# Agent attention with a gated expert layer: a shorter way to the list of failed tokens, and the last answer laid among the last products

## The chip, the cores and the metric

The kernel runs on one core of a Trainium2 chip. The metric is the time of one execution on the device in microseconds (us), as the median of several runs. One core has a matrix engine (TensorE, PE in the profile, with PEld for its weight loads), three element-wise engines (VectorE or DVE, ScalarE or ACT, GpSimd or POOL), a sequencer that mostly issues transfers (SyncE or SP), and DMA queues. Each engine takes its own instructions in the order in which they are written, and engines wait for one another through semaphores.

## What is computed

There are 4 batches of 11456 tokens, 128 channels and 49 agents. Each token's row is routed to one of 8 experts and goes through that expert's two layers (128 to 1024 to 128). The reference, cut to what matters:

```python
def _attn_ref(q, k, v, agents):
    a2k = sm(agents, k);  agent_v = a2k @ v          # sm: scaled softmax of a @ b.T
    return sm(q, agents) @ agent_v
def _moe_ref(x, expert_emb, tau, w1, w2):            # x: all 45824 rows
    ...
    expert_idx = np.argmax(logits, axis=1)
    gate_w = probs[np.arange(N), expert_idx]
    for e in range(E):
        mask = expert_idx == e
        h = np.maximum(x[mask] @ w1[e], 0.0)
        out[mask] = gate_w[mask, None] * (h @ w2[e])
```

## The kernel before

**Batches and units.** For each batch the kernel reads k and v and forms the agents' values. It then guesses one expert for the whole batch (`pick_expert`) and folds that expert's first layer into the space of the 49 agent scores: `gh` and `gl` are the folded weights that are kept, `lin` holds what could be taken as linear, `w2p` the second layer. GpSimd makes a factor `gts` of these (L946, L948), and TensorE multiplies it into `linp` (L952). Query tokens go by in units of up to 8 tiles of 128. A unit's scores become exponentials `e` and, transposed, `tt`. From there the batch's own layers run: a pair of products `hp` (L1338, L1339) for four tiles, ACT's `hh` (L1347) and DVE's `hh` (L1348), then for each tile the products `lin` (L1361) and twelve triples `yp` (L1373 to L1375), and for each group of tiles DVE's gated `ot` (L1389) and a store on ACT's queue (L1395).

**Failed tokens.** The folded form is only good for a token that is of the batch's guessed expert and for which the hidden units that were left out behave as assumed. `proved` tests the second: products `vp` (L1182, L1185), a sum on ACT (L1191), a minimum on DVE (L1188), collected in `vmin` and `vsum`. Once all tests of a batch are seen, `mark_strays(b)` runs. It finds each token's expert (`idx`), marks failed tokens (`odd`), and of the failed ones with the batch's own expert takes up to 5 of each partition with one sort of the largest 8 (`top`). A product with a triangular matrix (`had`, L1246) counts how many lie in the partitions before, so each picked token gets one of 128 places. Five comparisons make one-hot masks `mput` (L1272), and five products `mine` (L1281) move number and gate to those places. `fix(b)` turns the numbers to row indices `ix` (L1500), gathers the 128 q rows by an indirect transfer on POOL (`gather`, L1422) and calls `answer`.

**The answer.** `answer` computes 128 tokens in full: transpose `sqT` (L1431), scores `ssp` (L1437), softmax, transpose `seT` (L1449), attention rows `sx` (L1456), the expert's first layer `shp` (16 products at L1473, relu `sh` on ACT), second layer `syp` (16 products, L1479), the gate (`so`, L1484), and a scatter on POOL over the rows already stored (L1487). Every step but the first layers of batch 3 can stand among another batch's products; `w1s` and `w2s` are loaded anew. Tokens of another expert are counted by groups (`lga` L1308, `cnt_p` L1311, the transposes `mT` and `mB` at L222 and L228, `left`) and answered by `stray`, and those beyond that in a device loop at the end, which is entered only if some are left.

**What sets the order.** All these parts are Python generators. `spawn` enters one in a list that is advanced at each step of the loop over TensorE's products, `yield n` waits n steps, `urgent(g, k)` advances g k times a step at a high priority, and `in_place(y_last)` makes the scheduler place a product behind the last own product written so far. So a change in a count of steps, or in when a generator is spawned, moves instructions on every engine.

Of the kernel before, what the change touches and what calls it, by code (L numbers as in the profile page):

```python
# [29 lines left out]
def kernel(ctx: ExitStack, tc: tile.TileContext, q, k, v, agents, emb, tau, w1, w2, out):  # L30
# [18 lines left out]
    KEEP = 5  # L49
    LATE = 16  # L50
# [280 lines left out]
    def setup():  # L331
# [4 lines left out]
        with tc.issue_after(turned[0].ins):  # L336
            pool.iota(iotaf, pattern=[[1, FV]], base=0, channel_multiplier=0, allow_small_or_imprecise_dtypes=True)
            pool.iota(uid, pattern=[[P, NF]], base=0, channel_multiplier=1)
            pmem(half, 0.5)
            pool.iota(iota8m, pattern=[[1, E]], base=64, channel_multiplier=0, allow_small_or_imprecise_dtypes=True)  # L340
            pool.iota(iota8n, pattern=[[1, E]], base=-LO, channel_multiplier=0, allow_small_or_imprecise_dtypes=True)
            pool.iota(pidx, pattern=[[0, 1]], base=0, channel_multiplier=1, allow_small_or_imprecise_dtypes=True)
            dve.tensor_scalar(tri, iotaf[:, :P], pidx, None, ALU.is_gt)
            dve.tensor_tensor(out=fold, in0=ident[:, :A], in1=ident[:, LO : LO + A], op=ALU.add)
            dve.tensor_reduce(out=mrow[:, :1], in_=fold, axis=AX.X, op=ALU.add)
            dve.tensor_scalar(mrow[:, 1:], mrow[:, :1], -1.0, 1.0, ALU.mult, ALU.add)
            pmem(iotah, -1.0)
            pool.tensor_copy(iotah[:, :P], iotaf[:, :P])
            pool.tensor_copy(iotah[:, P + XA :], iotaf[:, P:FN])
            pool.iota(tok[:, :, :J], pattern=[[N, B], [1, J]], base=0, channel_multiplier=J,  # L350
                      allow_small_or_imprecise_dtypes=True)
        yield 1
        with tc.issue_after(turned[0].ins):
            pool.iota(tok[:, :, J:], pattern=[[N, B], [1, REM_J]], base=P * J, channel_multiplier=REM_J,
                      allow_small_or_imprecise_dtypes=True)
        pmem(gid, -1.0)
# [378 lines left out]
    def pick_expert(b, g):  # L735
# [23 lines left out]
        dve.tensor_copy(bt.e0, e0i)  # L759
# [337 lines left out]
    def route_group(b, gi, n):  # L1097

        bt = batches[b]
        if gi == 0:  # L1100
            bt.lg = wk.tile([P, NCOL, E], F32, name="lga", tag="lga", bufs=1)
            bt.es = es_all[:, b, :]
            bt.l = sm.tile([P, NCOL], F32, name="la", tag="la")
            bt.vmin = sm.tile([P, NCOL], F32, name="vmin", tag="vmin")
            bt.vsum = sm.tile([P, NCOL], F32, name="vsum", tag="vsum")
            bt.seen = 0
            pmem(bt.vmin, BIG)
            pmem(bt.vsum, 0.0)
# [34 lines left out]
        act.activation(ex, lg, AF.Exp)  # L1143
        yield 1
# [55 lines left out]

    def mark_strays(b):

        bt = batches[b]
        while bt.seen < sum(len(checks(b, u)) for u in range(NU)):
            yield 1
        yield 2
        dve.scalar_tensor_tensor(out=bt.lg, in0=bt.lg, scalar=0.0, in1=iota8n.unsqueeze(1).broadcast_to([P, NCOL, E]),
                                 op0=ALU.is_equal, op1=ALU.mult)
        yield 1
        idx = sm.tile([P, NCOL], F32, name="idx", tag="idx", bufs=1)  # L1210
        dve.tensor_reduce(out=idx, in_=bt.lg, axis=AX.X, op=ALU.min)
        yield 1
# [3 lines left out]
        ne = sm.tile([P, NCOL], F32, name="ne", tag="ne", bufs=1)  # L1216
        dve.tensor_tensor(out=ne, in0=bt.l, in1=bt.l, op=ALU.mult)
        yield 1
        dve.scalar_tensor_tensor(out=ne, in0=bt.qq[:, 1], scalar=bt.far, in1=ne, op0=ALU.mult, op1=ALU.is_ge)
        yield 1  # L1220
        dve.scalar_tensor_tensor(out=odd, in0=bt.vmin, scalar=0.0, in1=ne, op0=ALU.is_lt, op1=ALU.max)
# [5 lines left out]
        dve.tensor_scalar(ne, idx, float(LO), bt.e0, ALU.add, ALU.not_equal)  # L1227
        yield 1
        dve.tensor_tensor(out=odd, in0=ne, in1=odd, op=ALU.is_lt)
        pmem(odd[REM_P:, J:], 0.0)  # L1230
        yield 1
        cand = sm.tile([P, NCOL], F32, name="mine", tag="mine", bufs=1)
        top = sm.tile([P, 8], F32, name="top", tag="top", bufs=1)
        had = sm.tile([P, 8], F32, name="had", tag="had", bufs=1)
        cnt = sm.tile([P, 1], F32, name="had1", tag="had1", bufs=1)
        c16 = sm.tile([P, 1], F16, name="had16", tag="had16", bufs=1)
        dve.scalar_tensor_tensor(out=cand, in0=tok[:, b], scalar=1.0, in1=odd, op0=ALU.add, op1=ALU.mult)
# [3 lines left out]
        dve.tensor_scalar(had[:, :KEEP], top[:, :KEEP], 0.0, 0.0, ALU.is_gt, ALU.add, accum_out=cnt)  # L1241
        yield 1
# [5 lines left out]
        own = sm.tile([P, 1], F32, name="had3", tag="had3", bufs=1)  # L1248
        dve.tensor_tensor(out=own, in0=t_[:, :1], in1=cnt, op=ALU.add)
        dve.tensor_copy(cnt, t_[:, :1])  # L1250
        yield 1
        dve.tensor_scalar(had[:, :KEEP], iotaf[:, :KEEP], cnt, None, ALU.add)
# [5 lines left out]
        pick = sm.tile([P, KEEP, 2], F32, name="mpick", tag="mpick", bufs=1)  # L1258
        dve.tensor_copy(pick[:, :, 0], top[:, :KEEP])
        yield 1  # L1260
        mg = sm.tile([P, NCOL], F32, name="mgate", tag="mgate", bufs=1)
        mj = bt.vmin
        dve.tensor_tensor(out=mg, in0=bt.es, in1=odd, op=ALU.mult)
        yield 1
        for i in range(KEEP):
            dve.scalar_tensor_tensor(out=mj, in0=cand, scalar=top[:, i : i + 1], in1=mg, op0=ALU.is_equal, op1=ALU.mult,
                                     accum_out=pick[:, i, 1:])
            yield 1
        parts = sm.tile([P, KEEP, 3, 2], F16, name="mparts", tag="mparts", bufs=1)
        puts = sm.tile([P, B * NCOL], F32, name="mput", tag="eq", bufs=1).bitcast(F16)[:, : KEEP * P].rearrange("p (k f) -> p k f", f=P)  # L1270
        for i in range(KEEP):
            dve.tensor_scalar(puts[:, i], iotaf[:, :P], had[:, i : i + 1], None, ALU.is_equal)  # L1272
        for i in range(3):
            pool.tensor_copy(parts[:, :, i], pick)
            if i < 2:
                pool.tensor_tensor(out=pick, in0=pick, in1=parts[:, :, i], op=ALU.subtract)
        yield 3
        t_ = pss("mine")
        with in_place(y_last):
            for i in range(KEEP):  # L1280
                pe.matmul(out=t_[:, :6], lhsT=puts[:, i], rhs=parts[:, i].rearrange("p i w -> p (i w)"), start=(i == 0), stop=(i == KEEP - 1))  # L1281
# [10 lines left out]
        spawn(fix(b), 1, half=True)  # L1292
# [134 lines left out]
    def answer(xq, ix, gt, aT, avn, w1s, w2s, tiles=0):  # L1427
# [62 lines left out]
    def fix(b):  # L1490
# [5 lines left out]
        none = sm.tile([P, 1], F32, name="none", tag="none", bufs=1)  # L1496
        ix = sm.tile([P, 1], I32, name="ix", tag="ix")
        dve.tensor_scalar(none, bt.fix[:, :1], 0.5, 2 * BIG, ALU.is_lt, ALU.mult)
        yield 1
        dve.scalar_tensor_tensor(out=ix, in0=bt.fix[:, :1], scalar=-1.0, in1=none, op0=ALU.add, op1=ALU.add)  # L1500
# [4 lines left out]
        yield from answer(xq, ix, bt.fix[:, 1:], aT_all[:, b], av_all[:, b], w1s, w2s, (b + 1) * NT)  # L1505
        bt.fixed = True

    def stray():
# [23 lines left out]
        dve.tensor_copy(ix, mv)  # L1532
# [52 lines left out]
        yield from answer(xq, ix, gt, aT, avn, w1s, w2s)  # L1585
# [290 lines left out]
```

## Time and profile before

| quantity | value |
|---|---|
| time, median of 3 runs | 665.69 us (664.45 to 666.1) |
| the profiled execution's own time | 663.57 us |
| its span in the trace | 661.8 us |
| mean granted TensorE clock | 0.991 |
| busy: PE, DVE, ACT, POOL | 622.5, 501.5, 460.5, 354.4 us |

The table says that TensorE is busy for 94% of the span, so a gain has to come from its waits, from the stretch at the end in which it waits for the answer's chain, or from its own work. Busy times of matrix products are modelled at their ends, so a busy TensorE may still lose time; what the stretches show is read from the rows below.

### The profile page before, as it was taken

How to read it: one execution, taken by the hardware profiler on the slowest of the kernel's cores; microseconds unless marked ns; L12 is line 12 of the kernel's file. 1: busy time of each engine (PE TensorE's matmuls, PEld its weight loads, DVE VectorE, ACT ScalarE, POOL GpSimd, SP SyncE). 2: the span in 40 equal slices, each digit the busy share in tenths (PEclk: the TensorE clock that was granted, in tenths of full speed). 3: DMA queues.
4: the chain of work that ended last, by engine and by line, in shares of the span. 5: the costliest groups of instructions: out<-in, count | busy, mean ns of one | idle time of the engine just before them, and what ended most of it. 6: DMA issues, size and time to landing. Idle time of an engine off the chain costs nothing. (4 is left out here: it accounts for less than half of the span.)

```text
span 661.8 us, 22215 instructions
## 1 busy us (share of the span) xinstructions
PE 622.5 (94%) x8738; PEld 534.1 (81%) x8738; DVE 501.5 (76%) x1451; ACT 460.5 (70%) x1159; POOL 354.4 (54%) x639
## 2 busy tenths in 40 slices
PE   8998989999999899999999979999989898999994
PEld 6887878878888688888888768888878787888774
DVE  5775789787887888567798997645776999856892
ACT  3536855878679975877788956875687865789541
POOL 7003275474654666677345764767445768885110
PEclk9998899999999999999999999999998999999999
DMA  8997098399989559898969158996476325323321
GB/s 345 280 346 229 18 310 229 114 249 258 265 218 224 117 131 258 217 288 202 265 159 301 51 121 215 272 265 156 145 169 176 99 58 131 94 58 128 118 109 59
DMA packets 157045, 123.23 MB, mean 186 GB/s; under 512 B 76758, under 2 KB 133160, under 8 KB 156940
## 3 DMA queue, kind: packets, MB, share of 16 engines
q1 hardware_dynamic: 143499, 97.97, 58.5%
q10 hardware_dynamic: 13120, 23.47, 10.5%
q8 instruction: 69, 1.13, 0.7%
q0 software_dynamic: 320, 0.36, 0.2%
q14 instruction: 37, 0.29, 0.2%
HBM read 80.26 MB, written 23.79 MB: 157 GB/s over the span
## 5 line engine op out<-in xcount | busy, mean ns | idle before, releaser
L1191 ACT ACTIVATE vp<-vp 128x512 f32<-128x512 f32 x180 | 106.6, 592 | 11.4 <-PE vp L1182 9.8
L1370 PE MATMUL yp<-w2f,hh 128*128 128x128 f32 (+1 forms) x696 | 95.0, 278 | 0.0
L462 PE MATMUL half<-aT_all,fT 128*64 128x49 f32 x2304 | 86.1, 225 | 2.7 <-DVE vm L996 1.2
L1370 PEld LDWEIGHTS yp<-w2f,hh 128*128 128x128 f32 (+1 forms) x696 | 86.1, 191 | 2.6
L462 PEld LDWEIGHTS half<-aT_all,fT 128*64 128x64 f32 x2304 | 76.5, 139 | 11.9 <-issue 2.4
L1347 ACT ACTIVATE hh<-hp 128x512 f16<-128x512 f32 (+1 forms) x94 | 54.4, 588 | 40.4 <-PE hp L1339 25.7
L454 ACT COPY fT<-fTp 128x512 f32<-128x512 f32 (+1 forms) x115 | 63.5, 569 | 19.0 <-PE fTp L449 15.7
L1348 DVE SCALAR_TENSOR_TENSOR hh<-hp,hh 128x512 f16<-128x512 f32 (+1 forms) x94 | 63.1, 676 | 16.9 <-ACT hh L1347 16.7
L1389 DVE TENSOR_TENSOR ot<-yp,gs 128x512 f32<-128x512 f32 (+1 forms) x92 | 61.6, 669 | 17.9 <-PE yp L1370 12.5
L1338 PE MATMUL hp<-tt,gh 128*128 128x512 f16 (+1 forms) x184 | 69.0, 375 | 3.8 <-DVE rt L1087 1.5
L1373 PE MATMUL yp<-w2p,hh 128*128 128x128 f16 x372 | 70.2, 220 | 0.5 <-ACT hh L1347 0.5
L1374 PE MATMUL yp<-w2p,hh 128*128 128x128 f16 x372 | 70.2, 220 | 0.0
L1375 PE MATMUL yp<-w2p,hh 128*128 128x128 f16 x372 | 69.4, 220 | 0.0
L1182 PE MATMUL vp<-vm,tt 128*128 128x256 f16 x360 | 67.2, 273 | 1.9 <-ACT vp L1191 1.4
L1339 PE MATMUL hp<-tt,gl 128*128 128x512 f16 (+1 forms) x184 | 68.9, 375 | 0.0
L1129 POOL TENSOR_TENSOR nrm<-qq,half 128x16 f32<-128x16 f32 (+2 forms) x28 | 68.6, 2450 | 0.4
L1343 ACT ACTIVATE hh<-hp 128x512 f32<-128x512 f32 (+1 forms) x90 | 51.7, 579 | 14.9 <-PE hp L1339 11.0
L449 PE MATMUL fTp<-ident,qt 128*128 128x128 f32 x360 | 54.2, 280 | 0.9 <-ACT vp L1191 0.6
L1054 POOL CAST e<-qe 128x240 f16<-128x240 f32 (+1 forms) x48 | 18.9, 393 | 58.3 <-ACT qe L1045 39.9
L1090 POOL TENSOR_TENSOR rt<-rt 128x384 f32<-128x384 f32 (+1 forms) x48 | 40.7, 848 | 16.6 <-DVE rt L1087 15.3
L604 PE MATMUL half<-vt,kd 128*64 128x129 f32 x720 | 47.6, 277 | 1.0 <-issue 0.7
L1053 POOL TENSOR_TENSOR e<-qe,e 128x392 f16<-128x392 f32 (+1 forms) x48 | 42.2, 878 | 12.0 <-ACT e L1050 11.2
(392 smaller groups left out, 1703.3 us busy)
## 6 DMA issues: line engine op xcount, KB each, us to landing
kt<-in_k_dram SPq DMA_DIRECT2D x44, 512.0 KB, 6.4
vt<-in_v_dram SPq DMA_DIRECT2D x44, 512.0 KB, 6.3
qt<-in_q_dram SPq DMA_DIRECT2D x44, 512.0 KB, 6.1
out_dram<-ot ACTq DMA_DIRECT2D x88, 256.0 KB, 3.3
w1s<-in_moe_w_dram SPq DMA_DIRECT2D x9, 512.0 KB, 4.2
w2s<-in_moe_w_dram SPq DMA_DIRECT2D x9, 512.0 KB, 6.6
tt<-e SPq DMA_TRANSPOSE x48, 4.4
kt<-in_k_dram SPq DMA_DIRECT2D x4, 96.0 KB, 8.8
```

The costliest lines, as they stand in the source:

```text
L454: act.copy(dst, tp[:, : m * p])
L462: i = pe.matmul(out=s[h : h + w, c * A : (c + 1) * A], lhsT=xT[:, c * p + h : c * p + h + w], rhs=aT_all[:, b, :], start=True, stop=True, ...
L1129: pool.tensor_tensor(out=nrm, in0=quad, in1=half[:, :n], op=ALU.pow)
L1182: pe.matmul(out=z[:p, i * FP : (i + 1) * FP], lhsT=tt[:, c * p : (c + 1) * p], rhs=bt.vm[:, NEAR:], start=True, stop=True)
L1191: act.activation(z[:p], z[:p], AF.Relu, scale=-1.0, accum_out=bt.vsum[:p, at : at + 1])
L1338: pe.matmul(out=hp[:, :m], lhsT=bt.gh[:, fs], rhs=tt, start=True, stop=False)
L1339: pe.matmul(out=hp[:, :m], lhsT=bt.gl[:, fs], rhs=tt, start=False, stop=True)
L1348: dve.scalar_tensor_tensor(out=hl[:, :m], in0=hp[:, :m], scalar=0.0, in1=hh[:, :m], op0=ALU.max, op1=ALU.subtract)
L1370: y_last[:] = [pe.matmul(out=y, lhsT=hh[:, cs], rhs=bt.w2f[:, f], start=False, stop=last, skip_group_check=True)]
L1373: pe.matmul(out=y, lhsT=hh[:, cs], rhs=wh, start=False, stop=False, skip_group_check=True)
L1374: pe.matmul(out=y, lhsT=hh[:, cs], rhs=wl, start=False, stop=False, skip_group_check=True)
L1375: y_last[:] = [pe.matmul(out=y, lhsT=hl[:, cs], rhs=wh, start=False, stop=last, skip_group_check=True)]
```

## The change

Token numbers are stored as 4·11456 minus the number, so 0 means none. The token's own-expert test times its number (`own_e`) is made before the last test comes in. After the last test there follow: two marks into `odd`, one product with `own_e`, the sort, a 5-column mask `c16`, the `had` product (now 5 columns), a sum, one comparison for all five masks (128x640, over overlapping windows of one ramp), five products with the numbers alone (`mids`), a sum, the index `mix`, the gather. Gates are picked and moved by five more products (`mparts`) after that, and the answer takes them through a function. For the last batch the search for experts is split in two (`nearest`), the tests and the marking are spawned earlier, and the two layers of the last answer wait until all own tiles have been recorded and are tied to the last own product. For the other batches the answer's weights are loaded 34 steps after the gather, not 24.

```diff
+        final = b == B - 1 and gi == len(groups) - 1
+        if final:
+            jobs.extend((b, u, cs) for u in groups[gi] for cs in checks(b, u))
...
+        if final:
+            spawn(urgent(mark_strays(b), RUSH_MARK), half=True)
...
-        for u in groups[gi]:
+        for u in groups[gi] if not final else []:
             jobs.extend((b, u, cs) for cs in checks(b, u))
-        if gi == len(groups) - 1:
-            spawn(mark_strays(b) if b < B - 1 else urgent(mark_strays(b), 4), 1, half=True)
+        if b == B - 1 and gi == len(groups) - 2:
+            spawn(nearest(b, 0, ucol(groups[-1][0])), 1, half=True)
+        if b < B - 1 and gi == len(groups) - 1:
+            spawn(mark_strays(b), 1, half=True)
...
+        dve.scalar_tensor_tensor(out=own_e, in0=idx, scalar=bt.e0, in1=tok[:, b], op0=ALU.is_equal, op1=ALU.mult)
...
+        while bt.seen < sum(len(checks(b, u)) for u in range(NU)):
+            yield 1
         dve.scalar_tensor_tensor(out=odd, in0=bt.vmin, scalar=0.0, in1=ne, op0=ALU.is_lt, op1=ALU.max)
...
-        dve.scalar_tensor_tensor(out=cand, in0=tok[:, b], scalar=1.0, in1=odd, op0=ALU.add, op1=ALU.mult)
+        dve.tensor_tensor(out=cand, in0=odd, in1=own_e, op=ALU.mult)
         yield 1
         dve.max(out=top, in_=cand)
         yield 1
-        dve.tensor_scalar(had[:, :KEEP], top[:, :KEEP], 0.0, 0.0, ALU.is_gt, ALU.add, accum_out=cnt)
-        yield 1
-        dve.tensor_copy(c16, cnt)
+        dve.tensor_scalar(c16, top[:, :KEEP], 0.0, 0.0, ALU.is_gt, ALU.add, accum_out=own)
+        ids = sm.tile([P, KEEP, 2], F16, name="mids", tag="mids", bufs=1)
+        pool.tensor_copy(ids[:, :, 0], top[:, :KEEP])
+        pool.tensor_tensor(out=ids[:, :, 1], in0=top[:, :KEEP], in1=ids[:, :, 0], op=ALU.subtract)
         yield 1
         t_ = pss("had")
-        pe.matmul(out=t_[:, :1], lhsT=tri, rhs=c16, start=True, stop=True)
...
+        pe.matmul(out=t_[:, :KEEP], lhsT=tri, rhs=c16, start=True, stop=True)
+        yield 1
+        dve.tensor_reduce(out=cnt, in_=t_[:, :KEEP], axis=AX.X, op=ALU.add)
+        yield 1
...
+        dve.tensor_scalar(puts, ahead, float(KEEP - 1), cnt, ALU.subtract, ALU.is_equal)
...
+        t_ = put(ids, 2)
+        yield 1
+        ix = sm.tile([P, 1], I32, name="mix", tag="mix", bufs=2)
+        dve.tensor_reduce(out=top[:, KEEP : KEEP + 1], in_=t_[:, :2], axis=AX.X, op=ALU.add)
+        dve.tensor_scalar(ix, top[:, KEEP : KEEP + 1], -1.0, float(B * N), ALU.mult, ALU.add)
+        yield 1
+        spawn(fix(b, ix) if b < B - 1 else urgent(fix(b, ix), RUSH), 0 if b == B - 1 else 1, half=True)
...
-        for i in range(KEEP):
-            dve.tensor_scalar(puts[:, i], iotaf[:, :P], had[:, i : i + 1], None, ALU.is_equal)
...
+        t_ = put(parts, 3)
...
-        while not room():
+        while not room() or tiles == B * NT and len(stored) < tiles:
             yield 1
...
-                pe.matmul(out=t_[:, i * P : (i + 1) * P], lhsT=w1s[:, f * P : (f + 1) * P], rhs=x, start=True, stop=True)
+                with in_place(y_last if tiles == B * NT else []):
+                    pe.matmul(out=t_[:, i * P : (i + 1) * P], lhsT=w1s[:, f * P : (f + 1) * P], rhs=x, start=True, stop=True)
...
         xq = gather(ix)
-        yield 24 if b < B - 1 else 0
+        yield 34 if b < B - 1 else 0
```

On TensorE at the program's end, before the change, the last own products (`yp`) are followed by the whole answer of batch 3; `mB` is the count's transpose:

```order
L1375 LDWEIGHTS hh
L1375 MATMUL yp<-w2p,hh 96x128
L228 MATMUL mB<-ident,mTx 128x32
L1431 MATMUL sqT<-ident,xq 128x128
L1437 MATMUL ssp<-aT_all,sxT 128x49
L1449 MATMUL seT<-ident,se 49x128
L1456 MATMUL sx<-seTs,av_all 128x128
L1473 MATMUL shp<-sx,w1s 128x128 x8
L1479 MATMUL syp<-w2s,sh 128x128 x8
```

After the change this part stands on TensorE some six and a half tiles earlier, right behind `mT` and a pair `hp`, with one more pair `hp` in it (lines have moved by about 40):

```order
L230 MATMUL mB<-ident,mTx 128x32
L1471 MATMUL sqT<-ident,xq 128x128
L1378 LDWEIGHTS gh
L1378 MATMUL hp<-tt,gh 128x512
L1379 LDWEIGHTS gl
L1379 MATMUL hp<-tt,gl 128x512
L1477 MATMUL ssp<-aT_all,sxT 128x49
L1489 MATMUL seT<-ident,se 49x128
L1496 MATMUL sx<-seTs,av_all 128x128
L1401 LDWEIGHTS tt
L1401 MATMUL yp<-lin,tt 128x128
```

The end of TensorE's own products is then, after the change:

```order
L1414 LDWEIGHTS hh
L1414 MATMUL yp<-w2p,hh 96x128
L1415 LDWEIGHTS hh
L1415 MATMUL yp<-w2p,hh 96x128
L1516 MATMUL shp<-sx,w1s 128x128 x8
L1522 MATMUL syp<-w2s,sh 128x128 x8
```

The four small products and `mB` have moved ahead of the last tiles, and `shp` directly follows the last `yp`.

GpSimd around the factor `gts` of batch 3's folded layer, before (`rt`, `lga`, `la`, `ls`, `nrm` are parts of the routing of a group of units):

```order
L1140 TENSOR_TENSOR lga<-lga,cc 128x80
L946 TENSOR_TENSOR gts<-gts,mask 128x8x15 x2
L948 TENSOR_TENSOR gts<-gts,mask 128x8x49
L1152 TENSOR_SCALAR el<-es_all 128x10
L1131 TENSOR_SCALAR la<-rtg 128x8
L948 TENSOR_TENSOR gts<-gts,mask 128x8x49
```

and after:

```order
L1146 TENSOR_TENSOR lga<-lga,cc 128x80
L1056 TENSOR_TENSOR e_0_150<-qe,e_0_150 128x8x49
L1160 TENSOR_SCALAR el<-es_all 128x10
L1161 TENSOR_TENSOR el<-el,la 128x10
L1137 TENSOR_SCALAR la<-rtg 128x8
L1138 TENSOR_TENSOR ls<-la,sg_9248 128x8
L132 MEMSET lga 32x16
L1093 TENSOR_TENSOR rt<-rt 128x16x24
L1142 TENSOR_TENSOR lga<-rtg,rmx 128x64
L949 TENSOR_TENSOR gts<-gts,mask 128x8x15 x2
L951 TENSOR_TENSOR gts<-gts,mask 128x8x49
L1133 TENSOR_SCALAR qq<-qq 128x8
```

Five steps of the next group's routing and two of the last one's (`el`) now stand ahead of the first `gts`, all of which were behind it before. Behind `qq` follow `rt` and only then the last `gts`.

## Rows read from the trace of the kernel before

**Rows 1.** Stretches: window, length, PE, PEld, DVE, ACT, POOL busy (count), PEclk, DMA share, GB/s
```profile
494.00:497.00 3.00, 0.49 (x3) 0.22 (x4) 0.92 (x2) 1.65 (x4) 0.00 (x0) 0.88 1.12 249
497.00:500.00 3.00, 3.00 (x32) 2.72 (x31) 1.15 (x10) 2.38 (x5) 0.67 (x3) 0.55 1.07 374
...
540.00:555.00 15.00, 13.77 (x194) 12.38 (x194) 14.93 (x60) 8.27 (x25) 10.50 (x16) 1.00 0.49 125
...
620.00:625.00 5.00, 4.07 (x43) 2.71 (x42) 3.23 (x10) 2.82 (x7) 0.09 (x1) 1.00 0.15 56
625.00:630.00 5.00, 5.00 (x70) 4.05 (x68) 5.00 (x18) 2.11 (x4) 0.00 (x0) 1.00 0.28 108
...
648.00:652.00 4.00, 2.03 (x10) 1.29 (x10) 1.81 (x9) 1.36 (x6) 0.00 (x0) 1.00 0.30 104
652.00:656.00 4.00, 3.69 (x32) 3.50 (x31) 0.21 (x1) 1.20 (x2) 0.00 (x0) 1.00 0.02 4
```

**Rows 2.** Timeline of PE at the end: start, length, work, [idle before, releaser]
```profile
645.50 0.38 PE L1361 MATMUL yp<-lin,tt 128*128 128x128 f16 x4 [0.77 <-DVE ot L1389]
...
647.79 0.22 PE L1375 MATMUL yp<-w2p,hh 128*96 128x128 f16 x1
647.94 0.40 PE L228 MATMUL mB<-ident,mTx 32*128 32x32 f32 x2
648.27 0.33 PE L1431 MATMUL sqT<-ident,xq 128*128 128x128 f32 x1
648.96 0.42 PE L1437 MATMUL ssp<-aT_all,sxT 128*128 128x49 f32 x2 [0.35 <-ACT sxT L1434]
650.29 0.31 PE L1449 MATMUL seT<-ident,se 128*49 128x128 f32 x1 [0.91 <-ACT se L1446]
650.95 0.49 PE L1456 MATMUL sx<-seTs,av_all 49*128 49x128 f32 x2 [0.35 <-ACT seTs L1453]
651.79 2.05 PE L1473 MATMUL shp<-sx,w1s 128*128 128x128 f32 x16 [0.35 <-ACT sx L1459]
```

**Rows 3.** Timeline of DVE, ACT's queue and POOL at the end
```profile
641.51 0.14 DVE L1500 SCALAR_TENSOR_TENSOR ix<-fix,none 128x1 int32<-128x1 f32 x1
...
642.77 0.89 DVE L1311 TENSOR_REDUCE cnt_p<-lga 128x8 f32<-128x720 f32 x1
...
648.70 0.34 ACTq L1395 DMA_DIRECT2D out_dram<-ot  x1
...
641.93 1.10 POOL L1422 DMA_INDIRECT xq<-in_q_dram,ix  x1 [2.92 <-DVE ix L1500]
656.41 1.03 POOL L1487 DMA_INDIRECT out_dram<-so,ix  x1 [13.38 <-DVE so L1484]
```

**Rows 4.** DMA issues, with their median time from issue to landing
```profile
out_dram<-ot ACTq DMA_DIRECT2D x88, 256.0 KB, 3.3
...
xq<-in_q_dram,ix POOLq DMA_INDIRECT x5, 4.8
```

**Rows 5.** Timeline of PE at two earlier waits
```profile
392.13 2.05 PE L952 MATMUL linp<-w2s,gts 128*128 128x128 f32 x16 [3.01 <-POOL gts L948]
...
623.10 0.38 PE L1338 MATMUL hp<-tt,gh 128*128 128x512 f16 x1 [0.44 <-DVE hh L1348]
```

**Rows 6.** Two tiles, batch 3: count: ns min/median/max, first to last start
```profile
L1272 DVE TENSOR_SCALAR mput<-iotaf,had x5: 248/248/249, 635.0 to 635.6; 128x128 f16<-128x128 f16 x5
...
L1281 PE MATMUL mine<-mparts,mput x5: 165/167/168, 636.2 to 636.5; 128*128 128x6 f16 x5
```

**Rows 7.** Timeline of POOL, then PE, around batch 3's folded layer
```profile
525.25 0.85 POOL L948 TENSOR_TENSOR gts<-gts,mask 128x392 f32<-128x392 f32 x1
526.05 0.21 POOL L1153 TENSOR_TENSOR el<-el,la 128x10 f32<-128x10 f32 x1
...
528.14 0.84 POOL L1086 TENSOR_TENSOR rt<-qe 128x392 f32<-128x392 f32 x1
...
526.15 2.05 PE L952 MATMUL linp<-w2s,gts 128*128 128x128 f32 x16
```

More of the change, by code (lines that the diff above doesn't have):

```diff
@@ L1199, in prove, with nearest @@
             proved(*jobs.pop(0))
+    def nearest(b, c0, c1):
+        bt = batches[b]
+        while c0 == 0 and b > 0 and not hasattr(batches[b - 1], "marked"):
+            yield 1
+        lg = bt.lg[:, c0:c1]
+        dve.scalar_tensor_tensor(out=lg, in0=lg, scalar=0.0, in1=iota8n.unsqueeze(1).broadcast_to([P, c1 - c0, E]),
+                                 op0=ALU.is_equal, op1=ALU.mult)
+        yield 1
+        idx = sm.tile([P, NCOL], F32, name="idx", tag="idx", bufs=1) if c0 == 0 else bt.idx
+        dve.tensor_reduce(out=idx[:, c0:c1], in_=lg, axis=AX.X, op=ALU.min)
+        bt.idx = idx
+        yield 1
     def mark_strays(b):
         bt = batches[b]
-        while bt.seen < sum(len(checks(b, u)) for u in range(NU)):
-            yield 1
[L1206 to L1212, printed above, removed]
+        if b < B - 1:
+            while bt.seen < sum(len(checks(b, u)) for u in range(NU)):
+                yield 1
+            yield 2
+            yield from nearest(b, 0, NCOL)
+        else:
+            while not hasattr(bt, "idx"):
+                yield 1
+            yield from nearest(b, ucol(groups[-1][0]), NCOL)
+        idx = bt.idx
         while b < B - 1 and not hasattr(batches[b + 1], "vm"):
@@ L1220, in mark_strays @@
         yield 1
+        while bt.seen < sum(len(checks(b, u)) for u in range(NU)):
+            yield 1
         dve.scalar_tensor_tensor(out=odd, in0=bt.vmin, scalar=0.0, in1=ne, op0=ALU.is_lt, op1=ALU.max)
@@ new lines, in mark_strays, with put @@
+        ahead = bass.AP(tensor=iotaf.tensor, offset=iotaf.offset, ap=[list(iotaf.ap[0]), [1, KEEP], [1, P]])
+        dve.tensor_scalar(puts, ahead, float(KEEP - 1), cnt, ALU.subtract, ALU.is_equal)
+        yield 1
+        def put(parts, w):
+            t_ = pss("mine")
+            with in_place(y_last):
+                for i in range(KEEP):
+                    pe.matmul(out=t_[:, :w], lhsT=puts[:, KEEP - 1 - i], rhs=parts[:, i], start=(i == 0), stop=(i == KEEP - 1))
+            return t_
@@ new lines, in mark_strays @@
+        for _ in range(RUSH_MARK):
+            yield 4
+        pick = sm.tile([P, KEEP], F32, name="mpick", tag="mpick", bufs=1)
+        mj = bt.vmin
+        for i in range(KEEP):
+            dve.scalar_tensor_tensor(out=mj, in0=cand, scalar=top[:, i : i + 1], in1=bt.es, op0=ALU.is_equal, op1=ALU.mult,
+                                     accum_out=pick[:, i : i + 1])
+            yield 1
+        dve.scalar_tensor_tensor(out=pick, in0=top[:, :KEEP], scalar=0.0, in1=pick, op0=ALU.is_gt, op1=ALU.mult)
@@ L1253, in mark_strays @@
+        parts = sm.tile([P, KEEP, 3], F16, name="mparts", tag="mparts", bufs=1)
+        for i in range(3):
+            pool.tensor_copy(parts[:, :, i], pick)
+            if i < 2:
+                pool.tensor_tensor(out=pick, in0=pick, in1=parts[:, :, i], op=ALU.subtract)
+        yield 1
+        dve.tensor_tensor(out=own, in0=own, in1=cnt, op=ALU.add)
+        dve.tensor_scalar(ne, idx, bt.e0, None, ALU.not_equal)
         yield 1
@@ L1495, in fix @@
             yield 1
[L1496 to L1500, printed above, removed]
         xq = gather(ix)
-        yield 24 if b < B - 1 else 0
+        yield 34 if b < B - 1 else 0
         w1s, w2s = load_expert(bt.e0i)
         yield 0 if b < B - 1 else 8
-        yield from answer(xq, ix, bt.fix[:, 1:], aT_all[:, b], av_all[:, b], w1s, w2s, (b + 1) * NT)
+        yield from answer(xq, ix, lambda: getattr(bt, "fix", None), aT_all[:, b], av_all[:, b], w1s, w2s, (b + 1) * NT)
         bt.fixed = True
@@ L1584, in stray @@
             yield 1
-        yield from answer(xq, ix, gt, aT, avn, w1s, w2s)
+        yield from answer(xq, ix, lambda: gt, aT, avn, w1s, w2s)
     def stray_first():
```

78 lines of the change are left out of this document (29 added, 49 removed).

## The prediction

> **What bounds the kernel now.** Start with the busy shares: TensorE works for 94% of the span, so only its waits, its own work and the end can pay. Then take the stretches. From 625 us TensorE and VectorE are both full (5.00 of 5.00 each), so the tail before the last own product has no free place on either [rows 1]. From 540 to 555 VectorE has 14.93 of 15.00 and TensorE 13.77: 1.23 us are lost there to a full VectorE. From 620 to 625 TensorE has 4.07 of 5.00, so 0.93 us go, of which one wait of 0.44 is for VectorE's `hh` [rows 1, 5]. Last, follow TensorE's timeline at the end. The last own product starts at 647.79; then comes a chain of small products with a wait before nearly each, and the answer's first layer `shp` starts at 651.79 [rows 2]. From 648 to 652 TensorE works 2.03 of 4.00 us [rows 1]. The scatter that closes the kernel starts at 656.41 [rows 3], and its landing ends the span of 661.8. So the answer's chain of 4.0 us stands bare at the end, and behind it `shp`, `syp` and scatter, which the change leaves in series.
>
> **The end: what goes.** The order shows `shp` directly behind the last `yp`, with its operand `sx` made six tiles earlier. From last own product to `shp` is now 651.79 − 647.79 = 4.00 us; it becomes one product's pace, some 0.1. That is a gain of **3.9**, provided that `sx` is long done, and six and a half tiles make it so.
>
> **The front: what comes back.** `mB`, `sqT`, `ssp`, `seT` and `sx` aren't removed; they stand in line on TensorE, which starts them and waits as before. The order puts a pair `hp` between `sqT` and `ssp` and nothing between `ssp`, `seT` and `sx`. So of the chain 647.94 to 651.79 = 3.85 us, the last wait of 0.35 (before `shp`) is now filled by own products, and the wait of 0.35 before `ssp` is covered by the pair `hp` [rows 2]. The rest, 3.85 − 0.70 = 3.15, is paid inside the stretch that was full. Could other engines make it cheaper? VectorE can catch up in these waits, but what follows on TensorE needs TensorE's own time, and all of it was used. Could they make it dearer? `mB` waits for VectorE's `mTx`, with only a pair `hp` between: up to 0.3; ACT's queue has three stores between `pm` and `se`, at 0.34 each like the one shown [rows 3], if they wait in front of the softmax: up to 1.0. Bounds: 2.8 (`mB` and its 0.33 covered as well) to 4.4; I take **3.1**, near the row itself, since the stores' `ot` are made some steps earlier.
>
> The front also needs the gathered rows early: `sqT` waits for the gather on POOL. Before, index to gather issue was 641.93 − 641.51 = 0.42, and the gather landed in 4.8 by its median [rows 3, 4]; together 5.2. Behind `mix` VectorE has four small operations, two large ones like `cnt_p` (0.89) [rows 3], two `hh`, `so` and `mTx` before `mB`: by the spacing of such rows about 4.5. So the wait is 0 to 1.0. One gather is not the median, and the large operations may be held up; I take 0 and keep 1.0 for the range.
>
> **The links.** The five masks at 0.248 become one operation over 640 [rows 6]. It costs no less than one of them and no more than the five, and the five start within 0.6 us, so it isn't dearer than 0.7 or cheaper by more than 0.6. Four or five operations of a single column go per batch. Where VectorE is full this gives TensorE time: at most the 1.23 lost between 540 and 555, at least nothing; I take a third, **0.4**. The second product for the gates costs TensorE five products; the present ones start from 636.2 to 636.5 [rows 6], so **0.15** with a margin for its load.
>
> **Stalls in the tail.** `lin` waits 0.77 at 645.50 for `ot`, which stands on VectorE behind `cnt_p` (0.89) at 642.77 [rows 2, 3]. In the new order both large operations of the count come before the front, and batch 2's `shp` and `syp` stand near them on TensorE, which need no `hh`. I take the whole **0.77**; it is 0 if the same wait appears there. Of the 0.93 between 620 and 625 I take **0.3**: the marks are spread otherwise, but the order of `hh` and `hp` stays alike.
>
> **Sum.** 3.9 − 3.1 + 0.4 − 0.15 + 0.77 + 0.3 = 2.1 us. So the profiled execution of 663.57 would become 661.5; it ran 2.1 below the median of 665.69, so on the median I forecast 665.69 − 2.1 = **663.6**. A measurement of this kernel can tell 0.3%, or 2.0 us, from no change: faster begins below 663.7, slower above 667.7. The forecast lies barely on the faster side. By the bounds alone the terms give from 3.9 − 4.4 − 1.0 − 0.15 = −1.65 (a loss) to 3.9 − 2.8 − 0.15 + 1.23 + 0.77 + 0.93 = 3.9 (a gain).
>
> **Rival 1, the front gives back nearly all.** With stores ahead of the softmax (front 3.9) and a gather that lands 0.5 late, 2.1 − 0.8 − 0.5 = 0.8 is left: 664.9, within 0.3%. For it speaks that TensorE takes its work in order, so every late link stands before seven tiles; against it that the waits of the chain in the rows are short.
>
> **Rival 2, a late linear part in the middle makes it slower.** GpSimd's order changes before batch 3's `gts`. Seven instructions that stand behind the last `gts` before, from 526.05 to the end of the one at 528.14, in all 2.93 us, now stand ahead of it. `linp` starts at 526.15, 0.05 after `gts` ends at 526.10, so nothing covers a delay [rows 7]. A wait of that kind exists: 3.01 at 392.13 for `gts` [rows 5]. A long wait can also lower the clock: after 494 to 497 with TensorE at 0.49 of 3.00 us, the clock in the next 3 us is 0.55 [rows 1], near the lower of its two levels (1.2 of 2.4 GHz), which loses 3 × 0.45 = 1.35 us. Together 4.3 against the gain of 2.1: 665.69 + 2.2 = **667.9**, slower. It decides from a wait of 2.1 us on for a loss at all, and of 4.1 for one that can be told. Against it: GpSimd may reach that place earlier, since its other work and TensorE's own order there are reshuffled too. Half of it, 1.5 us, gives 665.1, the same.
>
> **Rival 3, the clock falls in the front.** The front gives TensorE waits in the midst of seven tiles. If the clock fell as after 497, the tiles behind would lose 1.35 [rows 1]: 2.1 − 1.35 = 0.75, or 664.9. Against it: the same chain, bare, with 2.03 busy of 4.00 from 648 to 652, left the clock at 1.00 in that stretch and in 652 to 656 [rows 1], and in line it has two pairs `hp` more. The Trainium skill, in "TensorE: Matmul & The Clock Gate" under "HAM oscillation — how this bites in real kernels", says that waits between groups of products put the array back to the low clock and that the next group starts cold. By that rule this change would pay 1.35 for the move; the trace agrees at 497 and disagrees at 652.
>
> **Rival 4, the end doesn't move as said.** The scatter also waits until all stores have landed. The last store is issued at 648.70 and by the median of 3.3 lands at 652.0 [rows 3, 4]; the scatter starts at 656.41, and without 3.9 it starts at 652.5. The margin is 0.5. If the last store takes over 1.5 us longer than the median, a further 1.0 is held: gain 1.1, 664.6.
>
> **Rival 5, more stalls close.** If 620 to 625 loses nothing (0.93) and 540 to 555 nothing (1.23), the gain is 2.1 + 0.63 + 0.83 = 3.6: 662.1. If the stretch from 494 to 500 is also reordered so that its 2.51 of idle time or its 1.35 of clock are partly saved, some 661.
>
> **How the numbers follow.** Forecast 0.42, of which 0.28 on the faster side and 0.14 within 0.3% (the sum lies near the border, and its known terms lean to more stalls closing). Rival 5: 0.18, faster. Rival 1: 0.11, rival 3: 0.04, rival 4: 0.06, rival 2 by half: 0.06, all within 0.3%. Rival 2 in full, or with the front's worst: 0.13, slower. That makes faster 0.46, same 0.41, slower 0.13. The range from 660.9 to 667.4 takes in rival 5 and the loss of 1.65 (667.3), and leaves out rival 2 in full and the far end of rival 5.
>
> **What would show it.** Right: `shp` starts about 0.1 us after the last `yp` starts; from `mT` to `sx` TensorE loses some 2.5 us of waits; `lin` doesn't wait on `ot` near the count; the scatter comes about 8.6 − 3.9 = 4.7 us after the start of the last own product. Wrong: `sqT` waits for the transfer, `linp` of batch 3 waits over 2 us for `gts`, the granted clock is below 1.00 after the front, or the scatter waits for a store. If the end is shorter by 3.9 and the time isn't, the front or the middle has taken it, and the stretches before 640 tell which.

## The result and the profile after

The changed kernel takes 672.86 us (median of 6 runs, 671.81 to 676.82) beside 665.07 us for the kernel before: a ratio of 1.0133, with an interval of 1.0085 to 1.0182. It is slower by 1.3%, some 8.8 us, where 663.6 was forecast. The profiled execution has a span of 670.1 us, 8.3 more than before. The busy line of its page says that TensorE does not have much more to do; of its 627.2 us, some 3 are the same products at half the clock (below).

```profile
PE 627.2 (94%) x8758; PEld 538.8 (80%) x8758; DVE 502.5 (75%) x1424; ACT 462.2 (69%) x1159; POOL 354.7 (53%) x644
```

TensorE's timeline of the changed kernel, at the front in line and at the end (columns as in [rows 2]):

```profile
639.00 0.33 PE L1471 MATMUL sqT<-ident,xq 128*128 128x128 f32 x1
...
642.21 0.42 PE L1477 MATMUL ssp<-aT_all,sxT 128*128 128x49 f32 x2 [2.02 <-ACT sxT L1474]
643.74 0.45 PE L1489 MATMUL seT<-ident,se 128*49 128x128 f32 x1 [1.11 <-ACT se L1486]
644.54 0.79 PE L1496 MATMUL sx<-seTs,av_all 49*128 49x128 f32 x2 [0.35 <-ACT seTs L1493]
645.27 0.61 PE L1401 MATMUL yp<-lin,tt 128*128 128x128 f16 x4
...
659.22 0.22 PE L1415 MATMUL yp<-w2p,hh 128*96 128x128 f16 x1
659.28 2.00 PE L1516 MATMUL shp<-sx,w1s 128*128 128x128 f32 x16
...
661.74 2.05 PE L1522 MATMUL syp<-w2s,sh 128*128 128x128 f32 x16 [0.46 <-ACT sh L1518]
```

The end did what was forecast: `shp` starts 0.06 us after the last `yp`, where 4.00 lay between them in [rows 2]. From the last own product to the end of the span it is now 670.1 − 659.22 = 10.9 us, before 661.8 − 647.79 = 14.0: a gain of 3.1. But the front stands from 639.00 to 645.27, 6.3 us, and the stretches show that it costs more than its own time (columns as in [rows 1]):

```profile
638.00:641.00 3.00, 1.92 (x12) 0.77 (x9) 1.47 (x6) 0.78 (x2) 1.05 (x1) 1.00 0.60 179
641.00:644.00 3.00, 0.68 (x3) 0.46 (x3) 0.53 (x4) 0.66 (x3) 0.00 (x0) 0.85 0.42 159
644.00:647.00 3.00, 2.65 (x20) 2.24 (x20) 1.50 (x4) 0.53 (x2) 0.00 (x0) 0.50 0.72 279
647.00:650.00 3.00, 3.00 (x31) 3.00 (x29) 1.97 (x3) 1.19 (x2) 0.00 (x0) 0.51 0.02 7
650.00:653.00 3.00, 3.00 (x40) 2.29 (x38) 1.89 (x3) 1.19 (x2) 0.00 (x0) 1.00 0.24 92
```

From 638 to 644 TensorE works 2.60 of 6 us, and no other engine works more than 2.0 of them: it is a chain that waits. Then the granted clock is 0.50 to 0.51 for 6 us in which TensorE works 5.65, so some 2.8 us of its work are lost. What the chain waits for stands on ACT and its queue, and on POOL:

```profile
641.89 0.27 ACT L1474 COPY sxT<-sqT 128x128 f32<-128x128 f32 x1 [2.60 <-DMA out_dram<-so,mix]
641.91 1.34 ACTq L1435 DMA_DIRECT2D out_dram<-ot  x3
...
656.75 3.58 ACTq L1435 DMA_DIRECT2D out_dram<-ot  x4
661.09 1.09 ACT L1518 ACTIVATE sh<-shp 128x512 f32<-128x512 f32 x2 [4.24 <-PE shp L1516]
...
638.37 1.05 POOL L1530 DMA_INDIRECT out_dram<-so,mix  x1 [4.33 <-DVE so L1527]
```

`sxT` is batch 3's small copy, and what ended its wait is the scatter of **batch 2's** answer, issued at 638.37 and landed 3.4 us later, at some 641.8. In the code, `so`, `sxT` and `sx` share one buffer, and all later stores to the output wait for the scatter too, since it may write any row. Before, that scatter stood at 618.49; the change moved it 20 us, into the front.

In the middle there is a second loss, which had nothing to do with the front. The stretch from 410 to 430 us of the changed kernel, and the wait in it:

```profile
410.00:430.00 20.00, 17.22 (x244) 14.85 (x243) 12.93 (x46) 14.54 (x40) 12.39 (x16) 1.00 0.98 240
...
422.19 0.20 PE L1072 MATMUL rtp<-r_hi,tt 128*128 128x58 f16 x1 [2.78 <-DMA tt<-e]
```

The same in the kernel before:

```profile
410.00:430.00 20.00, 19.53 (x286) 17.03 (x286) 15.07 (x57) 17.04 (x46) 15.31 (x22) 1.00 1.09 286
...
422.07 0.20 PE L1069 MATMUL rtp<-r_hi,tt 128*128 128x58 f16 x1 [0.47 <-DMA tt<-e]
```

TensorE works 2.3 us less there, because a transposed transfer is waited for.

How the 8.3 us divide can be read at the point behind which both kernels have the same products left but for a few: 644 records of TensorE before, 650 after. The kernel before comes to it at 598.6 us, the changed one at 602.5:

```profile
598.60:661.80 63.20, 53.34 (x644) 44.05 (x641) 44.26 (x124) 32.10 (x83) 11.57 (x28) 0.99 0.26 93
602.50:670.10 67.60, 56.70 (x650) 46.97 (x647) 43.91 (x119) 32.16 (x84) 12.71 (x29) 0.93 0.24 88
```

So in these two profiles 3.9 us are lost ahead of the tail and 4.4 in it. This point is called the 650 point below.

### The profile page after: what moved, and what is told of

Same layout as the page of the kernel before. It is cut to its first block, busy times and chain, and to the rows that moved or that the text cites. A ratio compares the mean times of both kernels' runs of the same rounds, so it can differ in the third digit from the quotient of the medians.

```text
span 670.1 us, 22215 instructions
## 1 busy us (share of the span) xinstructions
PE 627.2 (94%) x8758; PEld 538.8 (80%) x8758; DVE 502.5 (75%) x1424; ACT 462.2 (69%) x1159; POOL 354.7 (53%) x644
## 5 line engine op out<-in xcount | busy, mean ns | idle before, releaser
L1413 PE MATMUL yp<-w2p,hh 128*128 128x128 f16 x372 | 71.4, 222 | 0.0
L1414 PE MATMUL yp<-w2p,hh 128*128 128x128 f16 x372 | 71.1, 222 | 0.0
L1415 PE MATMUL yp<-w2p,hh 128*128 128x128 f16 x372 | 70.3, 222 | 0.0
```

Source lines behind the costliest of these rows:

```text
L1413: pe.matmul(out=y, lhsT=hh[:, cs], rhs=wh, start=False, stop=False, skip_group_check=True)
L1414: pe.matmul(out=y, lhsT=hh[:, cs], rhs=wl, start=False, stop=False, skip_group_check=True)
L1415: y_last[:] = [pe.matmul(out=y, lhsT=hl[:, cs], rhs=wh, start=False, stop=last, skip_group_check=True)]
```

## The experiments

All ratios are to the kernel before, run beside them. The kernel before had medians of 664.29 (first four), 664.46 (next four), 665.16 (next three) and 663.65 (last) there, so ratios are compared, not medians.

| run | median us | ratio and interval |
|---|---|---|
| the change | 672.86 | 1.0133 (1.0085 to 1.0182) |
| e1_own_buffer | 673.19 | 1.0170 (1.0120 to 1.0220) |
| e2_24_steps | 665.35 | 1.0029 (0.9993 to 1.0065) |
| e3_late_marking | 665.16 | 1.0043 (1.0011 to 1.0075) |
| e4_before_34 | 670.31 | 1.0123 (1.0076 to 1.0170) |
| e5_buffer_and_queue | 672.44 | 1.0141 (1.0085 to 1.0196) |
| e6_late_marking_queue | 666.35 | 1.0026 (1.0001 to 1.0052) |
| e7_before_queue | 662.73 | 0.9960 (0.9933 to 0.9988) |
| e8_late_24_queue | 666.11 | 1.0038 (1.0009 to 1.0067) |
| e9_no_scatter2 | 666.52 | 1.0028 (0.9996 to 1.0061) |
| e10_before_no_scatter2 | 663.41 | 0.9977 (0.9946 to 1.0009) |
| e11_24_queue | 668.42 | 1.0069 (1.0036 to 1.0102) |
| e12_before_queue15 | 660.93 | 0.9950 (0.9915 to 0.9984) |

### Is it the shared buffer?

```diff
-        o = sm.tile([P, D], F32, name="so", tag="sxT", bufs=1)
+        o = sm.tile([P, B * NCOL], F32, name="so", tag="eq", bufs=1)[:, :D]
```

> The changed kernel with one edit: the gated answer so of a batch lies in the buffer of the masks, no longer in the one that it shares with sxT and sx. Theory A: the 2.02 us wait of ssp is the landing of batch 2's scatter, which holds that buffer; it goes to under 0.3, and with it the fall of the clock to 0.50 behind the front (some 3.4 us lost), so 5.4 us faster than the changed kernel, some 667.5. Rival A2 (the other waits of the front, 1.11 and 0.35, lower the clock alone): the wait goes, the clock still falls, 2 us faster, some 671. Rival A3 (the wait is for the gathered rows, not for the buffer): nothing changes, 672.9.

No. The wait of `ssp` goes from 2.02 to 0.41, as theory A has it, and the time does not move. The wait has gone one link further. ACT and its queue, then TensorE, of this run:

```profile
640.95 0.82 ACTq L1435 DMA_DIRECT2D out_dram<-ot  x2
641.82 0.26 ACT L1493 COPY seTs<-seT 49x128 f32<-49x128 f32 x1 [1.76 <-DMA out_dram<-so,mix]
...
642.13 0.79 PE L1496 MATMUL sx<-seTs,av_all 49*128 49x128 f32 x2 [1.71 <-ACT seTs L1493]
```

Now a store stands on ACT ahead of `seTs`, and the store waits for the same landing. The clock still falls (0.74 on average from 637 to 650 us). Theory A named the right releaser and a holder that was only one of several; that the clock falls all the same is what rival A2 had.

### Is it the buffer and ACT's queue?

```diff
-        act.dma_start(out=dst, in_=o[:p, :n])
+        (sp if b == B - 1 and t >= NT - 12 else act).dma_start(out=dst, in_=o[:p, :n])
```

with the edit of e1_own_buffer.

> e1_own_buffer with the last 12 stores issued on SP's queue in place of ACT's. Theory C: batch 2's scatter holds the front twice, by the buffer shared with sxT and by the stores behind it, which wait for its landing on ACT's queue with the front's copies queued behind them. With both taken away no wait of the front is over 0.9 us and the clock stays at 1.00 behind it: some 5 us faster than the changed kernel, 667 to 668. Rival C2 (the front in line costs as much whatever holds ACT: its own waits of 0.3 to 0.9 are enough to lower the clock): 671 or more.

The front itself now runs clean: its waits are 0.41, 0.48 and 0.35. The time stays, and theory C falls as put; 671 or more is what rival C2 had. TensorE, VectorE and one stretch of this run:

```profile
639.35 0.48 PE L1496 MATMUL sx<-seTs,av_all 49*128 49x128 f32 x2 [0.35 <-ACT seTs L1493]
642.38 0.59 PE L1401 MATMUL yp<-lin,tt 128*128 128x128 f16 x4 [2.55 <-DVE ot L1429]
...
641.64 1.42 DVE L1429 TENSOR_TENSOR ot<-yp,gs 128x512 f32<-128x512 f32 x2 [2.36 <-DMA out_dram<-ot]
...
640.00:643.00 3.00, 0.62 (x7) 0.62 (x7) 1.32 (x2) 0.14 (x1) 0.00 (x0) 0.50 0.68 262
```

The own products behind the front wait in its place. The stores, wherever they are issued, wait for the scatter; so the three output tiles `ot` stay full, VectorE waits for a tile and `lin` for VectorE. Three holders, one landing.

The clock, however, does not fall behind this wait. In this run it goes to 0.50 at 639.89, just as `sx` ends (639.35 + 0.48 = 639.83), when the front has had only its own three waits of up to 0.48:

```profile
637.00:640.00 3.00, 1.65 (x7) 0.88 (x8) 1.34 (x9) 1.04 (x5) 0.04 (x1) 0.97 0.50 148
639.89:646.72 6.83, 4.34 (x42) 4.34 (x42) 3.19 (x5) 1.44 (x3) 0.00 (x0) 0.51 0.51 194
```

So rival C2 is not refuted: in this trace the front in line is followed by the lower clock although nothing holds it.

### The cause itself: batch 2's scatter taken out

```diff
+        if tiles != (B - 1) * NT:
             pool.indirect_dma_start(out=out, ...
```

in the changed kernel (e9) and in the kernel before (e10).

> The changed kernel without batch 2's scatter: the failed tokens of batch 2 are answered but not written, so the output lacks those rows. Theory D: that scatter, late among the last tiles, is the cause of the tail's loss, and the buffer, ACT's queue and the three output tiles are only three ways in which it holds the front; without it the order spreads the front by itself, no wait of the front is over 1 us, the clock stays at 1.00: 6 to 8 us faster than the changed kernel, 665 to 667. Rival (the early front itself costs, whatever the scatter): 670 or more.

> The kernel before without batch 2's scatter (those rows are not written), as the control of e9_no_scatter2. Theory D: the scatter cost the kernel before only the 0.93 us of waits at 622 and 623, so it is 0.5 to 1.5 us faster than before. Rival (the scatter costs in every order what it costs the changed kernel): 5 us or more faster.

The times are as theory D has them. Without the scatter the changed kernel goes from 1.0133 to 1.0028, 7.0 us. The order spreads the front by itself: `sqT` at 643.04, `ssp` at 645.03, `seT` at 648.15, `sx` at 649.92, own products between all of them, and TensorE has no gap and the full clock. Three stretches of this run:

```profile
640.00:643.00 3.00, 3.00 (x45) 2.64 (x42) 1.87 (x5) 1.38 (x3) 0.00 (x0) 1.00 0.57 166
643.00:646.00 3.00, 3.00 (x39) 2.48 (x39) 2.63 (x8) 1.26 (x4) 0.00 (x0) 1.00 0.51 183
...
649.00:652.00 3.00, 3.00 (x48) 2.77 (x46) 2.49 (x5) 1.52 (x5) 0.00 (x0) 1.00 0.22 87
```

Behind the 650 point the changed kernel takes 67.6 us (the row is above) and e9_no_scatter2 60.7:

```profile
604.80:665.50 60.70, 53.52 (x650) 44.52 (x647) 43.60 (x119) 31.75 (x84) 11.68 (x28) 0.98 0.27 97
```

The difference of 6.9 is the 7.0 of the medians. TensorE is idle 67.60 − 56.70 = 10.9 us in the changed kernel and 60.70 − 53.52 = 7.2 here, 3.7 less, and works 3.2 less for the same products, of which the clock is 2.8.

The run changes two things at once, though. TensorE's order is the changed kernel's up to 632 us; behind that the front no longer stands in line. So it shows that the scatter at this place costs the changed kernel 7 us, by its landing and by the order that is built around it. How much is the landing alone is not shown: no run keeps the front in line without the scatter, and e5_buffer_and_queue suggests that a front in line pays for the clock in any case.

In the kernel before, the scatter's removal is worth 0.2% with an interval that holds zero. Its trace has no wait left at 622, so there the scatter cost the 0.93 us lost at 622, or less than can be told; the 5 us of the rival are excluded.

### Two kernels that keep the scatter but not its place

```diff
-        yield 34 if b < B - 1 else 0
+        yield 24 if b < B - 1 else 0
```

> The changed kernel with 24 steps in place of 34 between gather and weights in batches 0 to 2. The order then spreads the front over some 250 rows of own products. Theory A: the front's waits (2.0, 1.1, 0.35) and the fall of the clock go, some 6.5 us faster than the changed kernel. Theory B (the 34 steps also cost in the middle, 380 to 530 us): a further 2 to 4 us, so some 663. Rival (the middle's loss comes from the shorter links and the other order, whatever the steps): only the tail's part comes back, some 666.5.

```diff
-        final = b == B - 1 and gi == len(groups) - 1
+        final = False
...
-        if b < B - 1 and gi == len(groups) - 1:
-            spawn(mark_strays(b), 1, half=True)
+        if gi == len(groups) - 1:
+            spawn(mark_strays(b) if b < B - 1 else urgent(mark_strays(b), RUSH_MARK), 1, half=True)
```

> The changed kernel with the tests and the marking of the last batch entered where they were before (not earlier); the order is the changed kernel's up to some 590 us, and behind that the front is spread among own products. Theory A: waits and clock of the front come back, some 6 us faster than the changed kernel, 667, and the time up to 590 us is as in the changed kernel (3 to 4 us behind the kernel before). Rival (a fall of the clock belongs to the end whatever the order): no more than 2 us faster, 671.

Each takes away one of the two edits that together put the scatter there, and each gives back 0.9 to 1.0% (6 to 7 us). The scatter moves from 638.37 to 628.24 and 623.53. With the late marking TensorE has no wait of 0.5 us in the tail but the one of `syp` on `sh`; with 24 steps two are left, 0.7 of `hp` for `hh` and, when the output tiles wait, this one, behind which the clock is at 0.50 from 635.4 to 638.8:

```profile
635.82 0.61 PE L1401 MATMUL yp<-lin,tt 128*128 128x128 f16 x4 [1.92 <-DVE ot L1429]
```

So neither early marking nor the 34 steps alone brings the front in line; the pair did. As in e9_no_scatter2, the front is spread in both, so these runs don't part the landing from the order either. Behind the 650 point e3_late_marking and e6_late_marking_queue (below) take 60.5 and 60.3 us, as e9_no_scatter2 does; e1_own_buffer and e5_buffer_and_queue take 66.8 and 67.4, as the changed kernel does. In the changed order batch 2's `sx` stands 439 rows behind its `seT` on TensorE, and in e3_late_marking, which is the same order up to some 590 us, 37. Why the scheduler leaves it that long was not tried.

Theory B, that 34 steps cost in the middle, gets nothing from these: e2_24_steps has the wait at 422 at 0.67, not 2.78, but other waits stand elsewhere, and it comes to the 650 point at 602.6, no earlier than the changed kernel. Its own runs are next.

### The 34 steps by themselves

In the kernel before, 24 to 34 and nothing else; and the late marking with stores on SP's queue, at 34 (e6) and at 24 (e8).

> The kernel before with 34 steps in place of 24, and nothing else. Theory B (the 34 steps cost in the middle): 2 to 4 us slower than before, 667 to 669. Rival (the steps cost nothing by themselves): within 1.5 us of before, 664 to 666.5.

> e3_late_marking with the last 12 stores on SP's queue. Theory C: the first relu of the last answer no longer stands behind four stores (0.5 us), and hh no longer stands behind a store that waits for batch 2's scatter: 0.5 to 1.5 us faster than e3_late_marking, 663.7 to 664.7. Rival (ACT's queue holds nobody there): the same as e3_late_marking, 665.2.

> e6_late_marking_queue with 24 steps in place of 34. Theory B (34 steps cost in the middle, as in e4_before_34): 2 to 4 us faster than e6_late_marking_queue, 661 to 662. Rival (what 34 steps do to the time depends on the order that comes out, not on the count): no more than 1 us either way from e6_late_marking_queue.

In the kernel before, 34 steps cost 1.2%, twice the upper figure of theory B, above all by a wait that no other kernel has. A stretch and the wait in e4_before_34:

```profile
561.00:567.00 6.00, 0.27 (x3) 0.00 (x0) 6.00 (x27) 0.53 (x1) 2.46 (x5) 0.57 1.15 242
...
567.09 0.23 PE L1069 MATMUL rtp<-r_hi,tt 128*128 128x58 f16 x1 [5.73 <-DMA tt<-e]
```

In the changed kernel's links with late marking, 34 and 24 give 1.0026 and 1.0038: no difference. So the count has no price of its own; what matters is the order that comes out of it, and theory B's rival holds. Against e3_late_marking, e6_late_marking_queue is 0.17% lower, inside both intervals: that ACT's queue still holds something there is not shown. Its trace speaks against it: `syp` waits 0.46 for `sh` with the stores on SP's queue too (the rows are below, under the end).

### What the same reading does for the kernel before

The 0.49 and 0.44 that TensorE waits near 622 in the kernel before belong to the same cause. ACT, its queue and POOL there:

```profile
621.34 0.34 ACTq L1395 DMA_DIRECT2D out_dram<-ot  x1
621.73 2.60 ACT L1347 ACTIVATE hh<-hp 128x512 f16<-128x512 f32 x5 [1.68 <-PE hp L1339]
...
618.49 1.18 POOL L1487 DMA_INDIRECT out_dram<-so,ix  x1 [4.53 <-DVE vmin L1188]
```

ACT is idle 1.68 us ahead of `hh`, which is put down to `hp`; but `hp` had been done, and a store stands between, on the queue, that waits for the scatter of 618.49. To test it, the last stores go to SP's queue: 12 of them in e7 (the store at 621 not among them), 15 in e12.

```diff
-        act.dma_start(out=dst, in_=o[:p, :n])
+        (sp if b == B - 1 and t >= NT - 15 else act).dma_start(out=dst, in_=o[:p, :n])
```

> The kernel before with the last 12 stores on SP's queue. Theory C: the waits of 0.49 and 0.44 at 622 and 623 are ACT's stall of 1.68 behind the store at 621.34, which waits for batch 2's scatter; they go, and three stores no longer stand before the softmax: 0.9 to 1.5 us faster than before. Rival (they are waits for hp): within 0.5 us of before.

> The kernel before with the last 15 stores on SP's queue (12 in e7_before_queue), so that the store that waits for batch 2's scatter near 621 us no longer stands on ACT's queue. Theory C: both waits of 0.49 and 0.44 at 622 go and the kernel is 0.9 to 2.5 us faster than before. Rival (the waits come from the order of hp and hh, not from the queue): the 0.44 wait stays as in e7_before_queue and the time equals that run's.

With 15 stores moved both waits are gone and TensorE is full there. A stretch of e12_before_queue15:

```profile
620.00:625.00 5.00, 5.00 (x64) 3.82 (x63) 5.00 (x16) 3.21 (x6) 0.09 (x1) 1.00 0.27 107
```

It is 0.5% faster than the kernel before (0.9950, 0.9915 to 0.9984), and so beats both kernels. With 12 the wait of 0.44 stays, as its rival had it, yet the time is 0.4% lower already, and e10_before_no_scatter2, which has neither wait, is only 0.2% lower. So these waits are not all of the gain, and where the rest lies isn't shown.

The same edit on e2_24_steps gave nothing:

> e2_24_steps with the last 12 stores on SP's queue: marking early, 24 steps, batch 2's scatter at some 628 us. Theory D: stores behind that scatter no longer hold ACT, but the three output tiles still wait for it, so the 1.9 us wait of lin on ot in e2_24_steps stays: 0 to 1.5 us faster than e2_24_steps, 664 to 665.4. Rival (ACT's queue was what held lin): the wait goes, 2 us or more faster, 663.

It came out at 1.0069, above e2_24_steps by 0.4% with intervals that overlap, a miss for both sides. In its trace `lin` still waits 2.5 us for `ot`, as theory D had it; why the time is not lower stays open.

## Why the prediction was wrong, step by step

**The end**: right in mechanism, 3.1 in place of 3.9. `syp` waits 0.46 for `sh`, so the scatter comes 664.47 − 659.22 = 5.25 us after the last own product, not 4.7; and scatter to end takes 670.1 − 664.47 = 5.6 us, against 5.4 from the scatter in [rows 3]. Four stores stand ahead of that `sh` on ACT's queue (3.58 us from 656.75), but they are not what delays it: in e6_late_marking_queue they stand on SP's queue, and TensorE and ACT read the same.

```profile
655.76 2.00 PE L1516 MATMUL shp<-sx,w1s 128*128 128x128 f32 x16
658.23 2.05 PE L1522 MATMUL syp<-w2s,sh 128*128 128x128 f32 x16 [0.46 <-ACT sh L1518]
...
657.58 1.08 ACT L1518 ACTIVATE sh<-shp 128x512 f32<-128x512 f32 x2 [3.80 <-PE shp L1516]
```

In both `sh` starts 1.8 us after `shp`, before the change 1.2; why is open.

Two steps failed, the front and the middle. **The front** was priced at 3.1, at most 4.4, and the clock behind it at nothing. It took 6.6 us from `mB` (638.67) to the next own product (645.27), 6.2 without the pair `hp`, of which 2.02 are the wait of `ssp` for the landing of batch 2's scatter, and 2.8 in clock behind it, 9.0 in all: 5.9 more than the sum has. The places were in the text (the stores on ACT, what `ssp` waits for), but their waits were priced by their own lengths, 0.34 a store. What the stores wait for was not asked: the order shows batch 2's scatter close ahead of them, and [rows 3] show only batch 3's. Of batch 2's answer the text said only that it fills TensorE near the count.

**The gather** was early enough: `sqT` has no wait, as taken.

**Rival 3** (the clock), at 0.04, took place together with the front's miss, and cost 2.8 where it had 1.35. The argument against it, that the same chain at 648 to 652 left the clock at 1.00 [rows 1], rested on one execution. In e12_before_queue15 the same bare chain, with the same waits, ends in this row, 2.96 us where [rows 2] have 2.05 for it:

```profile
649.43 2.96 PE L1473 MATMUL shp<-sx,w1s 128*128 128x128 f32 x16 [0.35 <-ACT sx L1459]
```

In e7_before_queue and e10_before_no_scatter2 it is 2.92 and 3.43. So the clock fell at this chain in three of four traces, and rival 3 deserved far more than 0.04. The Trainium skill, in "TensorE: Matmul & The Clock Gate" under "HAM oscillation — how this bites in real kernels", has the effect, waits that put the array back to the low clock; but its case is a loop with one long wait for a transfer ahead of each group, which the prediction left out. The traces go beyond it: the longest wait was 2.02 us in the changed kernel's front and 0.91 in the bare chain, and the clock fell all the same.

**Stalls**: `lin` no longer waits 0.77 beside the count, and 620 to 625 has no gap left (5.00 of 5.00): right, and more than the 0.3 taken. But the second was not closed; its cause, the scatter, moved to where it costs more.

**The links and the middle** are the second step that failed. The sum has 0.4 − 0.15 for them and no term for what the new order does to transfers and waits ahead of the tail. The 0.4 hoped for where VectorE is full did not show: from 540 to 580 TensorE is idle 3.7 us, before 3.1, though the work in the two windows is not quite the same. The 650 point says it better, since it can be read in every trace. Four traces with TensorE's order of before up to there (before, e7, e10, e12) come to it at 596.8 to 598.6 us, six with the changed order (the change, e1, e3, e5, e6, e9) at 600.1 to 606.6; by their means the new order is 4.7 us later. Of this the wait at 422 explains some 1.5: it is 1.65 to 2.78 in the six and 0.16 to 0.69 in the four. The rest was not placed, and no run takes the middle's loss away alone, so its cause stays open. With 24 steps it is there too (e2_24_steps 602.6, e8_late_24_queue 602.8).

**Rival 2** (`gts` late in batch 3) did not come: `linp` has no wait there.

**Together.** The sum of 2.1, less 5.9 for the front, 4.9 for links and middle and 0.8 for the end, and with 0.6 more from the stalls, is −8.9; 8.8 slower was measured. Where the scatter is out of the way, the tail does what was forecast of it (3.9 − 3.1 + 0.77 + 0.3 = 1.9): behind the 650 point e3, e6 and e9 take 60.3 to 60.7 us, before 63.2. The middle takes that back, so even with the tail mended (e9_no_scatter2, e2_24_steps) the change stands within 0.3% of the kernel before, not 2 us ahead of it.

## What to carry to other kernels

When a change moves a step that writes memory at indices (a scatter), list what is written to the same tensor behind it, on which queue those writes stand, which small copies stand behind them on that engine, and how many output tiles are left until the landing: each is a holder, and here to free one only passed the wait to the next. The price was part of the landing (3.4 us, of which one wait of 2.02 showed) where a chain with no slack lay, and half the clock behind the chain. When a change reorders a whole program, compare the two traces at a point with the same work left, in more than one trace of each: here half of the loss lay ahead of the moved chain. A wait put down to an engine that had long been done is to be looked for on the queue of the waiting engine.

## What the runs showed of the hardware

In the changed kernel, TensorE's 2.60 of 6 us from 638 to 644 were followed by 6 us at 0.50 of the clock, the lower of its two levels (1.2 of 2.4 GHz). e1_own_buffer and e5_buffer_and_queue have the same fall, from 641.08 and 639.89 on, after TensorE worked 1.45 and 1.71 of the 3 us ahead of it; e9_no_scatter2, with 20.00 of 20 from 636, has none. One and the same chain of small products with waits of 0.35, 0.91, 0.35 and 0.35 us is met by the fall in three traces (e7, e10, e12) and not in a fourth (before). The profiled executions also differ by low stretches that no order explains: from 60 to 80 us the mean clock is 0.83 in the kernel before and 0.91 in the changed one, with the same TensorE order there, and by 90 us the changed one is 2.0 us ahead. One profile is thus no ground for a difference of 2 us. The waits for the transposed transfer `tt` at one and the same place ran from 0.16 to 0.69 us in four kernels with the order of before, and from 1.65 to 2.78 in six with the changed order. Issue to landing took 6.2 us before (wait 0.47), and 5.9 (e1, 1.65), 6.2 (e3, 1.95) and 7.1 (the change, 2.78) in the new order: the order makes most of the wait, not the transfer's own time.
